# Moving integer weight additions to GpSimd and reordering the first pass of a fused attention and MLP kernel

## The chip, the cores and the metric

The kernel runs on one core of one Trainium2 chip. The metric is the device time of one execution in microseconds, as the median of several executions. A ratio is the mean time of one kernel's runs over the mean of the other's in the same rounds, so it is not quite the ratio of the medians beside it. Different sessions ran on different chips, and the kernel before had a median between 1010.2 and 1012.8 us on them; compare ratios, not medians, across sessions.

Engines: PE is TensorE, PEld its weight loads, DVE is VectorE, ACT is ScalarE, POOL is GpSimd. Tiles whose names end in `_ps` lie in PSUM, the others in SBUF, the two on-chip memories that the program uses. A TensorE pass is one matmul instruction; a slot is one step of TensorE's list, eight such passes in the first matmul, which start 1.73 us apart when nothing holds them up.

## The reference, cut to what matters

```python
kv  = einsum('bhsd,bhse->bhde', k, v)              # q, k, v: 8 x 8 x 576 x 64
o   = einsum('bhsd,bhde->bhse', q, kv)
x   = o / rms(o) * g_norm                          # reshaped to 4608 x 512
h   = x @ w_in                                     # 512 x 2048
g   = s * relu(h)**2 + b
out = g @ w_out                                    # 2048 x 512
```

The two weights arrive as 64-bit floats. The kernel turns them into 32-bit floats on the chip, in its first pass over the tokens.

## The kernel before: the parts that matter here

The tokens go through nine passes, `u = 0` to 8. Both matrix products are done with seven half-size products each (a Strassen scheme), so sums of weight blocks and of activations are needed. Only the first pass also converts weights, 16 blocks of 128 x 1024 words: ScalarE goes over a block twice (fold the high word, round the low one), VectorE shifts the high words and adds the low ones as integers.

```python
def shift_hi(i, dst):
    nc.vector.tensor_scalar(out=dst.bitcast(U32), in0=pairs(i)[:, :, 1],
                            scalar1=3, scalar2=None, op0=ALU.logical_shift_left)

def add_lo(i, dst):
    d = dst.bitcast(U32)
    nc.vector.tensor_tensor(out=d, in0=d, in1=pairs(i)[:, :, 0], op=ALU.add)
...
def join(n):                       # directly one after the other
    shift(n); plus(n)              # plus: add_lo, then send the next load
    if n >= FC // 2: column_sums(s - NS, lower)     # w_out: bias row
    elif lower: [sums() for sums in sums_w_in(s)]   # w_in: Strassen sums
...
# one unit of the first matmul: a result leaves PSUM through ScalarE and VectorE
def z2():
    mm1_product(2, u, s, ps, True)
    t = g_tile("a11")
    add(t, ps, st["r1"])           # VectorE, one input in PSUM, one in SBUF
    relu_sq(t)                     # VectorE, both inputs in SBUF
```

The w_out blocks alternate between upper and lower half, so the second matmul's first product, which needs only the upper half, comes after nearly all of them. The second matmul of the first pass starts with the rows `x1`; the first product there is called "the w_up product" below.

## Time and profile before

| | before |
|---|---|
| median of 3 runs | 1010.23 us (1010.13 to 1012.59) |
| span of the profiled run | 1009.0 us |
| w_up product starts | 97.99 us (12 of 32 TensorE passes), the rest from 103.62 us |
| z2 of the second token pass starts | 167.01 us |
| from there to the end | 842.0 us |

How to read it: the last row is the same in every kernel of this study (841.8 to 842.1 us), because TensorE has no gaps there. So the kernel's span is its second-pass start plus 842.0 us, and all that can change is how soon the first pass ends. The lines that show this are in the prediction.

### The profile page before, as it was taken

The numbers are of one execution on the slowest core, as the hardware profiler recorded it, in microseconds if no ns is written. First come the engines' busy times: TensorE is split into PE (matmuls) and PEld (weight loads), VectorE is DVE, ScalarE is ACT, GpSimd is POOL, SyncE is SP. The second block draws the span as 40 slices with busy tenths as digits, with TensorE's granted clock in tenths as the row PEclk, the third lists the DMA queues.
The fourth block names the chain that finished last, engine by engine and source line by source line (L and its number), as shares of the span: only waits on it lengthen the run. The fifth ranks groups of instructions, "written<-read, shape, count | busy, mean of one in ns | idle before, by whom it ended". The sixth has DMA issues, their size and how long they took to land.

```text
span 1009.0 us, 13489 instructions
## 1 busy us (share of the span) xinstructions
PE 969.8 (96%) x5794; PEld 850.8 (84%) x5794; DVE 459.4 (46%) x749; ACT 205.3 (20%) x354; POOL 1.6 (0%) x8
## 2 busy tenths in 40 slices
PE   4878899999999999999999999999999999999998
PEld 3657688888888888888888888888888888888887
DVE  1989853453344433452445234533453344433441
ACT  2646121212121112112121212021212111112100
POOL 0000000000000000000000000000000000000000
PEclk9989999999999999999999999999999999999999
DMA  9555945913253324522552265134303250323033
GB/s 251 173 193 197 265 152 116 252 67 129 81 134 90 125 73 138 134 98 84 153 136 84 84 167 136 43 125 126 84 6 134 72 165 1 125 73 136 1 125 83
DMA packets 75243, 121.46 MB, mean 120 GB/s; under 512 B 41904, under 2 KB 49072, under 8 KB 68016
## 3 DMA queue, kind: packets, MB, share of 16 engines
q1 hardware_dynamic: 72048, 118.90, 39.2%
q10 hardware_dynamic: 3136, 1.71, 0.8%
q8 instruction: 45, 0.74, 0.3%
q14 instruction: 14, 0.11, 0.0%
HBM read 103.81 MB, written 16.78 MB: 120 GB/s over the span
## 4 chain that ended last, share of the span: by engine, by line
PE 89%; DVE 6%; DMA 2%; ACT 2%; issue 1%; SPq 0%; DVEq 0%; ACTq 0%
PE x_ps L84 49%; PE y_ps L84 26%; PE z_ps L84 8%; PE qT_ps L321 2%; PE kv_ps L297 2%; PE xT_ps L361 1%; DMA kv_sb<-in_k_dram 1%; DVE a L183 1%; DMA w<-w_up 1%; DVE ws L186 1%; DMA q_sb<-in_q_dram 0%; DVE a L409 0%; DVE b_row L183 0%; DVE wb L179 0%; DVE a L186 0%
## 5 line engine op out<-in xcount | busy, mean ns | idle before, releaser
L84 PE MATMUL x_ps<-w_sb,a 128*128 128x256 f32 x768 | 172.3, 379 | 0.0
L84 PEld LDWEIGHTS x_ps<-w_sb,a 128*128 128x128 f32 x768 | 144.3, 190 | 18.9 <-issue 0.2
L84 PE MATMUL x_ps<-xs,ws 128*128 128x256 f32 x576 | 139.1, 385 | 11.2 <-ACT r L425 9.3
L84 PE MATMUL y_ps<-w_sb,a 128*128 128x256 f32 x640 | 143.4, 379 | 0.0
L84 PE MATMUL y_ps<-xs,wb 128*128 128x256 f32 x576 | 136.1, 379 | 0.0
L84 PEld LDWEIGHTS x_ps<-xs,ws 128*128 128x128 f32 x576 | 110.4, 192 | 28.3 <-ACT r L425 10.9
L84 PEld LDWEIGHTS y_ps<-w_sb,a 128*128 128x128 f32 x640 | 119.4, 190 | 15.2 <-issue 0.2
L425 ACT COPY r<-x_ps 128x512 f32<-128x512 f32 x108 | 63.3, 586 | 338.4 <-PE x_ps L84 323.2
L84 PEld LDWEIGHTS y_ps<-xs,wb 128*128 128x128 f32 x576 | 109.3, 190 | 15.1 <-DVE a L183 0.2
L183 DVE TENSOR_TENSOR a<-y_ps,r 128x512 f32<-128x512 f32 x72 | 49.5, 687 | 127.6 <-ACT r L425 127.5
L409 DVE SCALAR_TENSOR_TENSOR a<-a 128x512 f32<-128x512 f32 x108 | 74.8, 692 | 3.7
L84 PE MATMUL x_ps<-xT,wa 128*128 128x256 f32 x288 | 69.5, 385 | 0.2 <-DVE wa L179 0.2
L84 PE MATMUL x_ps<-xT,ws 128*128 128x256 f32 x288 | 68.9, 382 | 0.7 <-ACT r L425 0.7
L84 PE MATMUL z_ps<-xT,wa 128*128 128x256 f32 x288 | 68.0, 379 | 0.0
L497 DVE SCALAR_TENSOR_TENSOR or<-x_ps,s_col,b_row 128x256 f32<-128x256 f32 x54 | 25.9, 482 | 85.9 <-PE x_ps L84 85.9
L347 DVE TENSOR_REDUCE ss<-xn 128x8 f32<-128x512 f32 x36 | 24.6, 684 | 84.6 <-ACT xn L345 84.4
L84 PEld LDWEIGHTS x_ps<-xT,wa 128*128 128x128 f32 x288 | 55.9, 194 | 8.5 <-DVE wa L179 0.6
L458 DVE TENSOR_TENSOR a<-a 128x512 f32<-128x512 f32 x36 | 24.9, 692 | 82.0 <-ACT a L457 82.0
L84 PEld LDWEIGHTS x_ps<-xT,ws 128*128 128x128 f32 x288 | 54.1, 190 | 8.9 <-ACT r L425 1.1
L84 PEld LDWEIGHTS z_ps<-xT,wa 128*128 128x128 f32 x288 | 54.6, 190 | 7.4
L84 PE MATMUL x_ps<-w_sb,s 128*128 128x256 f32 x256 | 57.8, 380 | 0.0
L84 PEld LDWEIGHTS x_ps<-w_sb,s 128*128 128x128 f32 x256 | 47.6, 190 | 6.1 <-issue 0.2
(79 smaller groups left out, 770.2 us busy)
## 6 DMA issues: line engine op xcount, KB each, us to landing
w_sb<-w SPq DMA_DIRECT2D x56, 1024.0 KB, 4.9
kv_sb<-in_k_dram SPq DMA_DIRECT2D x32, 288.0 KB, 5.7
out_dram<-o SPq DMA_DIRECT2D x72, 128.0 KB, 2.3
q_sb<-in_q_dram SPq DMA_DIRECT2D x68, 128.0 KB, 5.5
w_raw<-in_moe_w_in_dram SPq DMA_DIRECT2D x8, 1024.0 KB, 6.4
w_raw<-in_moe_w_out_dram SPq DMA_DIRECT2D x8, 1024.0 KB, 4.9
kv_sb<-in_v_dram SPq DMA_DIRECT2D x28, 288.0 KB, 6.8
w<-w_up SPq DMA_DIRECT2D x4, 1024.0 KB, 7.4
```

The costliest lines, as they stand in the source:

```text
L84: nc.tensor.matmul(o, lhsT=lhsT, rhs=rhs, start=start, stop=stop, skip_group_check=True)
L183: nc.vector.tensor_tensor(out=o, in0=a, in1=b, op=ALU.add)
L186: nc.vector.tensor_tensor(out=o, in0=a, in1=b, op=ALU.subtract)
L297: nc.tensor.matmul(ps[r][l * HB : l * HB + HB, i, :], lhsT=kv[rows, 0, l, j, :], rhs=kv[rows, 1, l, j, :], start=(j == 0), stop=(j == R - 1),)
L321: nc.tensor.transpose(ps[:, p, :], q_in[c][:, 2 * p : 2 * p + 2, :], ident)
L347: nc.vector.reduce_sum(ss, st["xn"], axis=mybir.AxisListType.X)
L361: nc.tensor.transpose(ps[:, p, :], st["xn"][:, 2 * p : 2 * p + 2, :], ident)
L409: nc.vector.scalar_tensor_tensor(t, t, 0.0, t, ALU.max, ALU.mult)
L425: nc.scalar.copy(st[name], src)
L458: nc.vector.tensor_mul(t, t, t)
L497: nc.vector.scalar_tensor_tensor(o, ps, s_col, other, ALU.mult, ALU.add)
```

## The change

The intent: VectorE is the busiest engine of the first pass, and GpSimd does nothing. The change gives GpSimd 14 of the 16 integer adds; loads the upper half of w_out first and brings forward a product that needs only that half (`early_5`); computes the sums of the first pass as they come up rather than in a lump; orders the first loads so that q arrives between the halves of k and v and turns q there; and copies those turned q tiles with VectorE instead of ScalarE. The core of the diff, with cuts:

```diff
-    def add_lo(i, dst):
+    def add_lo(i, dst, engine):
         if wide:
             d = dst.bitcast(U32)
-            nc.vector.tensor_tensor(out=d, in0=d, in1=pairs(i)[:, :, 0], op=ALU.add)
+            engine.tensor_tensor(out=d, in0=d, in1=pairs(i)[:, :, 0], op=ALU.add)
...
-    blocks = conv_order() + [FC + i for i in conv_order()]
+    blocks = [i for s in range(NS) for i in (2 * s, NU + 2 * s)]
+    blocks += [FC + 2 * s for s in range(2 * NS)]
...
     def plus(n):
-        add_lo(blocks[n], place(n))
+        add_lo(blocks[n], place(n), nc.vector if n < 2 else nc.gpsimd)
         send_w()
...
-    for i in range(2):
-        load_kv(0, i, kv0p, (nc.sync, nc.scalar), tag="kv")
-    load_q(0)
-    load_q(2, nc.scalar)
+    both = (nc.sync, nc.scalar)
+    load_kv(0, 0, kv0p, both, tag="kv")
+    load_q(0, both)
+    load_kv(0, 1, kv0p, both, tag="kv")
+    load_q(2, both)
...
-    turn[0]()
-    turn[1]()
+    kv_product(0, lambda: [turn[c]() for c in range(2)])
...
-    turn_x[2]()
     first[0]["x1"]()
+    turn_x[2]()
+    first[0]["z2"]()
     turn_x[3]()
...
-    for sums in (t12, s12, t34, s34):
-        sums()
+    s12()
+    t12()
+    shift(2)
+    plus(2)
+    t34()
+    s34()
...
+    for n, slot in starts.items():
+        at(slot, (hi, n))
+        at(slot + 1, (lo, n), (shift, n), (plus, n))
+        at(slot + 4, (more, n))        # the sums that use block n, three slots later
...
+        if u == 0:
+            return [
+                lambda: x1(0),
+                seq(lambda: x1(1), s2),
+                lambda: early_5(0),
+                lambda: early_5(1),
+                seq(lambda: z2(0), with_bias),
+                ...
```

More of the change, by code (lines that the diff above doesn't have):

```diff
@@ L107, in halves, with load_q @@
         return [(b, i), (b, 4 + i)]
-    def load_q(c, queue=nc.sync):
+    def load_q(c, queues=(nc.sync, nc.sync)):
         t = qp.tile([P, 2, H, D], FP32, name="q_sb", tag="q")
@@ L113, in load_q @@
             for s, (b, j) in enumerate(halves(c + i)):
-                queue.dma_start(
+                queues[i].dma_start(
                     out=t[s * HB : s * HB + HB, i],
@@ L230 @@
     W2_AT = {
-        1: w_up[:, :, :HN], 6: w_up[:, :, :HN], 5: w_up[:, :, :HN], 7: w_up[:, :, HN:],
+        1: w_up[:, :, :HN], 7: w_up[:, :, :HN], 5: w_up[:, :, HN:],
         2: w_dn[:, :, :HN], 4: w_dn[:, :, :HN], 3: w_dn[:, :, HN:],
@@ L247, in column_sums, with sub_w_out @@
                 add(b_row, b_row, w[:, f])
-    def sum_w_out(i, fn, a, b):
-        for s in range(NS):
+    def sub_w_out(i, a, b, steps=range(NS)):
+        for s in steps:
             blocks = slice(2 * s, 2 * s + 2)
-            fn(W2_AT[i][:, blocks], W2_AT[a][:, blocks], W2_AT[b][:, blocks])
+            sub(W2_AT[i][:, blocks], W2_AT[a][:, blocks], W2_AT[b][:, blocks])
     def store_w2(*which):
@@ L285, in bias_row, with kv_product @@
         nc.scalar.copy(b_row, ps)
-    def kv_product(b):
+    def kv_product(b, between=lambda: None):
         ps = [ps_t.tile([P, 2, D], FP32, name="kv_ps", tag="t") for _ in range(2)]
         for i in range(2):
+            if i == 1:
+                between()
             kv = kv_in.pop((b, i))
@@ L318, in turn @@
         def turn():
-            ps = ps_t.tile([P, NP, P], FP32, name="qT_ps", tag="t")
+            if first and c == 0:
+                ps = ps_a.tile([P, NP, P], FP32, name="qT_ps", tag="x")
+            elif first and c == 1:
+                ps = bank_of("att", "z", 1).rearrange("p b (m n) -> p (b m) n", m=2)
+            else:
+                ps = ps_t.tile([P, NP, P], FP32, name="qT_ps", tag="t")
             for p in range(NP):
@@ L322, in turn @@
             st["qT"] = attp.tile([P, NP, P], FP32, name="qT", tag="qT")
-            nc.scalar.copy(st["qT"], ps)
+            if first:
+                nc.vector.tensor_copy(out=st["qT"], in_=ps)
+            else:
+                nc.scalar.copy(st["qT"], ps)
         def product():
@@ L459, in x3 @@
             g_tile("s1")
-            if u > 0:
-                g_sums(s)
+            g_sums(s)
         def y4():
@@ L524, in x1, with early_5, with_bias @@
                 part("r1", j, st["x", j], b1)
-        def first_parts():
-            if u == 0:
-                bias_row()
-                for j in range(2):
-                    part("r1", j, st["x", j], b1)
+        def early_5(j):
+            ps = half(("w", j), "y")
+            product(5, j, ps, True)
+            nc.scalar.activation(rows("o1", j)[:, HN:], ps, AF.Copy, scale=s_col)
+        def with_bias():
+            bias_row()
+            for j in range(2):
+                part("r1", j, st["x", j], b1)
+            for j in range(2):
+                add(st["o1", j][:, HN:], st["o1", j][:, HN:], b2)
+            scaled(st["o1", 0][:, :HN], st["z"], st["r1", 0])
         def z2(j):
@@ L534, in z2 @@
             product(2, j, ps, True)
-            scaled(rows("o1", j)[:, :HN], ps, st["r1", j])
+            if u == 0 and j == 0:
+                st["z"] = ps
+            else:
+                scaled(rows("o1", j)[:, :HN], ps, st["r1", j])
         def s2():
@@ L547, in x6 @@
             part("r2", j, st["x", j], b1)
+            if u == 0:
+                part("r4", j, st["x", j], st["o1", j][:, HN:])
         def y7(j):
@@ L551, in y7 @@
             product(7, j, st["y", j], True)
+            if u == 0:
+                scaled(rows("o2", j)[:, HN:], st["y", j], st["r4", j])
         def x5(j):
@@ L559, in x3 @@
             product(3, j, st["x", j], False)
-            scaled(rows("o1", j)[:, HN:], st["x", j], b2)
+            scaled(rows("o1", j)[:, HN:], st["x", j], b2 if u > 0 else st["o1", j][:, HN:])
             store("o1", j, 4 * u + j)
@@ L577, in nxt, with t3 @@
                 return (lambda: load_w2(u + 1, n - 7)) if u + 1 < U else (lambda: None)
-            return (lambda: None) if u == 0 else (lambda: load_w2(u, n))
-        def t2():
-            if u == 0:
-                sum_w_out(6, add, 7, 1)
-                store_w2(6)
-        def t4():
-            if u == 0:
-                sum_w_out(4, sub, 2, 6)
-                store_w2(4)
-        def t1():
-            if u == 0:
-                sum_w_out(5, sub, 3, 6)
-                store_w2(5)
+            return lambda: load_w2(u, n)
+        def t3():
+            sub_w_out(7, 6, 1)
+            store_w2(7)
+        def t4():
+            sub_w_out(4, 2, 6)
+            store_w2(4)
+        if u == 0:
+            return [
[4 more added lines that the diff above has]
+                seq(lambda: z2(0), with_bias),
+                seq(lambda: z2(1), t3, s4),
+                lambda: x6(0),
+                seq(lambda: x6(1), t4),
+                lambda: y7(0),
+                lambda: y7(1),
+                lambda: x3(0),
+                lambda: x3(1),
+                lambda: y4(0),
+                lambda: y4(1),
+            ]
         return [
             lambda: x1(0),
-            seq(lambda: x1(1), nxt(2), first_parts, t2, s2),
+            seq(lambda: x1(1), nxt(2), s2),
             lambda: z2(0),
-            seq(lambda: z2(1), nxt(3), s4, t4),
+            seq(lambda: z2(1), nxt(3), s4),
             lambda: x6(0),
-            seq(lambda: x6(1), nxt(4), t1),
+            seq(lambda: x6(1), nxt(4)),
             lambda: y7(0),
@@ L606, in mm2 @@
             lambda: x3(0),
-            seq(lambda: x3(1)),
+            lambda: x3(1),
             lambda: y4(0),
-            seq(lambda: y4(1)),
+            lambda: y4(1),
         ]
@@ L618, in tc_late @@
         late["kv"] = ctx.enter_context(tc.tile_pool(name="kvp", bufs=2, side="right"))
-    def conv_order():
-        return [i for s in range(NS) for i in (2 * s, NU + 2 * s)]
-    blocks = conv_order() + [FC + i for i in conv_order()]
+    blocks = [i for s in range(NS) for i in (2 * s, NU + 2 * s)]
+    blocks += [FC + 2 * s for s in range(2 * NS)]
     sent = [0]
@@ L629, in send_w, with where @@
             sent[0] += 1
+    def where(n):
+        return divmod(n, 2) if n < 2 * NS else divmod(n - 2 * NS, NS)[::-1]
     def place(n):
-        s, lower = divmod(n, 2)
-        return w_in_at(s, lower) if n < FC // 2 else w_out_at(s - NS, lower)
+        s, lower = where(n)
+        return w_in_at(s, lower) if n < 2 * NS else w_out_at(s, lower)
     def hi(n):
@@ L639, in lo @@
         round_lo(blocks[n])
-    def split(n):
-        hi(n)
-        lo(n)
     def shift(n):
@@ L648, in plus, with more @@
     def plus(n):
-        add_lo(blocks[n], place(n))
+        add_lo(blocks[n], place(n), nc.vector if n < 2 else nc.gpsimd)
         send_w()
-    def join(n):
-        shift(n)
-        plus(n)
-        s, lower = divmod(n, 2)
-        if n >= FC // 2:
-            column_sums(s - NS, lower)
+    def more(n):
+        s, lower = where(n)
+        if n >= 2 * NS:
+            column_sums(s, lower)
+            if not lower:
+                sub_w_out(5, 5, 1, [s])
         elif lower:
@@ L663 @@
     kv0p = tc.alloc_tile_pool(name="kv0p", bufs=2)
-    for i in range(2):
-        load_kv(0, i, kv0p, (nc.sync, nc.scalar), tag="kv")
-    load_q(0)
-    load_q(2, nc.scalar)
+    both = (nc.sync, nc.scalar)
[3 more added lines that the diff above has]
+    load_q(2, both)
     for _ in range(3):
         send_w()
-    kv_product(0)
-    kv0p.release()
-    gp = ctx.enter_context(tc.tile_pool(name="gp", bufs=NS))
     between = [
@@ L685 @@
     )
-    turn[0]()
-    turn[1]()
+    kv_product(0, lambda: [turn[c]() for c in range(2)])
+    kv0p.release()
+    gp = ctx.enter_context(tc.tile_pool(name="gp", bufs=NS))
     hi(0)
@@ L724, in side_of @@
         if u == 0:
-            side[2].insert(0, lambda: kv_product(1))
+            side = {
+                6: [lambda: kv_product(1)],
+                7: [turn[0]],
+                8: [product[0], turn[1]],
+                9: [turn_x[0], product[1], turn[2]],
+                10: [turn_x[1], product[2], turn[3]],
+                11: [turn_x[2], product[3]],
+                12: [turn_x[3]],
+                13: side[12],
+            }
         return side
@@ L735, in loads, with at @@
             load_q(4 * u + 6)
-    at_slot = {
-        0: [(split, 3)], 1: [(join, 2)], 2: [(join, 3), (split, 4)], 4: [(join, 4), (split, 5)],
-        6: [(join, 5), (split, 6)], 8: [(join, 6)], 9: [(split, 7)], 10: [(join, 7)],
-        12: [(split, 8)], 13: [(join, 8)], 14: [(split, 9)], 15: [(join, 9)], 17: [(split, 10)],
-        18: [(join, 10)], 19: [(split, 11)], 20: [(join, 11)], 21: [(split, 12)],
-        22: [(join, 12)], 23: [(split, 13)], 25: [(join, 13), (split, 14)], 27: [(join, 14)],
-    }
+    at_slot = {}
+    starts = {3: 1, 4: 4, 5: 6, 6: 9, 7: 11, 8: 14, 9: 16, 10: 19, 11: 21, 12: 24, 13: 26}
+    def at(n, *steps):
+        at_slot.setdefault(n, []).extend(steps)
+    for n, slot in starts.items():
+        at(slot, (hi, n))
+        at(slot + 1, (lo, n), (shift, n), (plus, n))
+        at(slot + 4, (more, n))
+    last_slot = 7 * NS
+    at(last_slot, (hi, 14), (lo, 14), (shift, 14), (plus, 14))
+    at(last_slot + 1, (hi, 15), (lo, 15), (shift, 15), (plus, 15))
     for u in range(U):
@@ L763 @@
         for n, slot in enumerate(slots):
-            if u > 0 or n > 0:
+            if u > 0 or n > 1:
                 slot()
@@ L772 @@
                     load_kv(kv_due[u + 1], i, late["kv"], tag="kv")
-        if u == 0:
-            split(FC - 1)
-            join(FC - 1)
-            for i in range(2):
-                load_kv(1, i, convp, tag="raw", bufs=3)
-            loads(0)
-            store_w2(1, 2, 3)
-            sum_w_out(7, sub, 3, 7)
-            store_w2(7)
-            for s in range(NS):
-                g_sums(s)
         second, side = mm2(u), side_of(u)
@@ L786 @@
             slot()
+            if u == 0:
+                run(at_slot.get(last_slot + n, []))
+                if n == 1:
+                    for i in range(2):
+                        load_kv(1, i, convp, tag="raw", bufs=3)
+                    store_w2(1)
+                    loads(0)
+                    store_w2(5)
+                elif n == 2:
+                    t2 = convp.tile([P, 4 * R * D], FP32, name="w_t2", tag="raw", bufs=3)
+                    W2_AT[6] = t2[:, : FC // 2 * HN].rearrange("p (f n) -> p f n", n=HN)
+                    for i in range(14, 16):
+                        more(i)
+                    sub_w_out(6, 3, 5)
+                    store_w2(3, 2, 6)
             if n == 0 and u > 0:
```

## The prediction

> **What bounds the kernel now.** I read the busy time by stretches first, then TensorE's waits, then the timeline around the longest one, then VectorE's groups. The stretches (columns: window, its length, busy us and instructions of PE, PEld, DVE, ACT, POOL, then granted clock, DMA share, GB/s):
>
> ```profile
> 0.00:35.00 35.00, 18.25 (x223) 16.26 (x224) 10.47 (x20) 15.99 (x28) 1.63 (x8) 1.00 0.84 229
> 35.00:60.00 25.00, 17.33 (x76) 13.81 (x75) 23.42 (x34) 12.36 (x15) 0.00 (x0) 0.94 0.58 195
> 60.00:105.00 45.00, 37.72 (x154) 31.26 (x154) 40.42 (x56) 24.32 (x28) 0.00 (x0) 0.92 0.58 190
> 105.00:125.00 20.00, 18.70 (x224) 15.30 (x223) 16.84 (x29) 2.81 (x7) 0.00 (x0) 0.92 0.98 271
> 125.00:165.00 40.00, 38.24 (x203) 33.75 (x202) 20.44 (x39) 7.39 (x14) 0.00 (x0) 1.00 0.41 126
> 165.00:1004.00 839.00, 839.00 (x4922) 740.32 (x4921) 347.35 (x577) 142.44 (x264) 0.00 (x0) 1.00 0.36 106
> ```
>
> From 165 us on, TensorE is busy 839.00 of 839.00 us at full clock; the change leaves that work as it is, so nothing can be won there. Everything lies in the first pass (165 us), where TensorE is busy 18.25 + 17.33 + 37.72 + 18.70 + 38.24 = 130.2 us and idle 34.8. Some 11 of those are the wait for the first k and v. The clock column adds about 0.06 x 25 + 0.08 x 45 + 0.08 x 20 = 6.7 us lost to a lower clock (a little less, as some of it fell in idle time). So the ceiling is near 35 - 10 + 6 = 31 us, 3% of 1010.
>
> In 35 to 105 us VectorE is the busy engine, 23.42 of 25 and 40.42 of 45 us. TensorE's waits there:
>
> ```profile
> PE kv_ps L297 <- DMA kv_sb<-in_v_dram: 11.9, 2, 11.1
> PE x_ps L84 <- ACT r L425: 10.0, 5, 4.6
> PE xT_ps L361 <- DVE xn L353: 3.2, 3, 1.8
> PE x_ps L84 <- DVE w_up L179: 2.9, 1, 2.9
> ```
>
> ACT is named for 10.0 us, but ACT is only the messenger. The timeline at the longest wait:
>
> ```profile
> 57.52 0.69 DVE L409 SCALAR_TENSOR_TENSOR a<-a 128x512 f32<-128x512 f32 x1
> 58.13 0.68 DVE L183 TENSOR_TENSOR a<-y_ps,r 128x512 f32<-128x512 f32 x1
> 58.85 0.69 DVE L409 SCALAR_TENSOR_TENSOR a<-a 128x512 f32<-128x512 f32 x1
> 58.90 0.59 ACT L425 COPY r<-x_ps 128x512 f32<-128x512 f32 x1 [4.04 <-DVE a L183]
> 59.54 3.78 PE L84 MATMUL x_ps<-xs,ws 128*128 128x256 f32 x8 [4.62 <-ACT r L425]
> ```
>
> ACT itself sat 4.04 us until VectorE had read the old r at 58.13, because VectorE was working off its queue; and the eight passes after the pause took 3.78 us where undisturbed ones start 1.73 us apart. So VectorE's queue is the bound from 35 us to about 130 us. What the change aims at is this group:
>
> ```profile
> L179 DVE CUSTOM_DVE_ANT_0 w_up<-w_raw,w_up 128x2048 uint16<-128x2048 uint16 x4 | 4.9, 1226 | 0.2
> L179 DVE CUSTOM_DVE_ANT_0 w_dn<-w_raw,w_dn 128x2048 uint16<-128x2048 uint16 x4 | 4.9, 1226 | 0.3
> L169 DVE TENSOR_SCALAR wa<-w_raw 128x1024 uint32<-128x1024 uint32 x4 | 2.7, 687 | 0.0
> L183 DVE TENSOR_TENSOR b_row<-b_row,w_dn 128x512 f32<-128x512 f32 x8 | 5.5, 692 | 0.3
> ```
>
> An exact integer add of one weight block costs VectorE 1.226 us, and there are 16.
>
> **What the Trainium skill says.** "GPSIMD Engine Reference", 4.1 Engine selection: a 32-bit integer add there is exact, so the result stays right; 3.1 Elementwise gives 4497 ns for a two-input add of 2048 elements. Half that is an estimate of 2.25 us for a block of 1024. No trace here shows it: GpSimd only runs 1.63 us of setup. "SBUF — State Buffer", Who interferes with whom: a VectorE instruction with two SBUF inputs, or in a 2-port mode, contends with a GpSimd instruction that reads SBUF, and the second to issue "fully blocks". Not testable in this trace, and the main doubt. "VectorE: DVE Perf Modes", the tier table: fp32 tensor_scalar from SBUF runs at 2x. The trace agrees for the shift: 1024 words in 687 ns, against 692 ns for a tensor_tensor of 512; so the shift is a 2-port one. "TensorE: Matmul & The Clock Gate", Part 1: an idle window of about 3.4 us halves the clock. The trace agrees: after the 4.62 us pause the pace fell to 3.78 against 1.89 us for eight passes; 2.38 and 2.88 us pauses were also followed by slow passes.
>
> **The change part by part.**
> 1. *Integer adds.* 14 of 16 leave VectorE: 14 x 1.226 = 17.2 us of its time; on GpSimd 14 x 2.25 = 31.5 us by the estimate, at one block per 2.4 TensorE slots of 1.73 us = 4.1 us. GpSimd itself keeps up. The sums using a block follow three slots (5.2 us) after its add, which tolerates an add of up to some 4 to 5 us.
> 2. *w_out upper half first.* The first product of the second matmul needs only the upper half. Before, lower blocks stand between: three shifts (2.1), three adds (3.7) and six column sums (4.2). After, a lower block's work falls under that product and under the w5 product, moved forward: four products of 3.45 us = 13.8 us of TensorE work that needs no lower block. The w5 subtractions (4 x 0.69 = 2.7) and three units' g sums (6 x 0.69 = 4.1) move in front of it.
> 3. *VectorE's work until the first product can run.* Before, durations between 34.5 and 103.5 us sum to 66.2 us in 69. After, counted off the program from the first z addition: 11 additions from PSUM (7.5), 11 relu-squares (7.6), 3 squares (2.1), 16 w_in sums (11.0), 4 x sums (2.7), 10 shifts (6.9), 8 column sums (5.2), 4 w5 subtractions (2.7), 6 g sums (4.1) = 49.8 us. At the same density that is 49.8 x 69/66.2 = 52 us, so the product starts near 34.5 + 52 = 86.5 us. TensorE's 26 slots from 37.4 give 37.4 + 26 x 1.73 = 82, so both fit together.
> 4. *From there to the next pass.* Fourteen half products (48.3), k^T v (2.3), bias and attention (some 7.5) are 58 us without pauses. TensorE's first pass would end at 144.5 instead of 165.3: **20.8 us won if GpSimd costs VectorE nothing**. Before, the stretch from 103.6 took 61.7 us with about 3 us of waits and 2 of half clock.
> 5. *First loads, q turned inside k^T v, qT copied by VectorE.* The first k^T v half can start perhaps 1 us before 11.1. But ACT's first weight fold waits for its block at 21.39 us and stands before the first Square (22.43) in ACT's order, in both kernels. So little comes through: the four turns off ACT (585 ns each; ACT was full, 5.00 of 5.00 us, in 25 to 30 us) against 4 copies on VectorE of about 0.65 and a z addition and relu-square (1.4 us) placed before the x sums. I count 0, plus or minus 1.5.
>
> **The rivals.**
> *A: the lock is total.* Of the 49.8 us, 42.3 are instructions with two SBUF inputs or in 2-port mode; only the PSUM additions (7.5) can lie beside GpSimd. Ten adds needed before the product take the port 10 x 2.25 = 22.5 us. 42.3 + 22.5 = 64.8, plus part of the 7.5 and handing over: about 68 us, product at 102 to 103 instead of 103.6. The later steps still save 2 to 4 us: 1006 to 1010. With an add of 3 us, 7.5 us more come on top: 1010 to 1016. For it: the skill's sentence. Against it: moving 17 us away to hold the port for 31 would be an odd thing to keep, and three slots of slack fit adds that are delayed but done.
> *B: no contention.* 1010 - 20.8 = 989.5, at best; with a few short waits 990 to 994.
> *C: another engine takes over.* ACT's two passes over a block (1.17 + 1.16 us) for 14 blocks and about 15 copies at 0.59 are some 42 us in 52: near, but not the bound. Weight loads: a buffer is held for load (6.4 us), two passes (2.3), shift (0.7) and add (2.25), 11.7 us; three buffers give one block per 3.9 us, just under 4.1. If adds stretch to 4 us it becomes 4.5 us per block, 12 x 0.4 = 5 us lost, so about 5 of the 20.8 go: 994 to 996.
>
> I expect partial contention, VectorE's 42 us stretched by about a quarter (10 us): 20.8 - 10 = 10.8 won. **999.5 us.** The range is 988 (B, early loads helping) to 1011 (A). Two per cent is 20.2 us, below 990.0: needs B nearly whole, 0.14. Slower than 1030.4 needs adds that stop VectorE far more than their own length: 0.03. Within 2%: 0.83.
>
> **What would show it.** The changed profile should have 14 GpSimd adds near 2.3 us each (start to start within one block), VectorE's 512-element sums still near 0.69 us if there is no lock and 1 to 3 us beside an add if there is; the first w_up product between 87 (B) and 103 us (A); no TensorE wait over 3.4 us and full clock after 40 us; the next pass starting between 145 and 163 us; 839 us unchanged after it. I am wrong if the first Square comes much before 22 us (then the first loads did matter), if adds take over 4 us, or if z2's wait for the last lower block opens a new gap.

## The result, and the profile after

The changed kernel took **1015.13 us** (1014.78 to 1017.43, 4 runs), beside 1010.62 us for the kernel before: ratio 1.0046, 95% interval 1.0026 to 1.0066. A repetition in the last session gave 1.0039 (1.0021 to 1.0057). So it is slower, by under half a per cent: within the 2% that the prediction gave a chance of 0.83, but on the other side of the kernel before. The forecast of 999.5 us and the range 988 to 1011 were both missed.

The two stretches that VectorE bounds, in the changed kernel, with the columns of the prediction's first view:

```profile
35.00:60.00 25.00, 20.03 (x74) 16.09 (x72) 19.44 (x25) 10.38 (x12) 7.80 (x3) 0.80 0.42 132
60.00:105.00 45.00, 33.73 (x128) 27.69 (x129) 44.24 (x50) 20.64 (x24) 18.15 (x7) 0.86 0.52 181
```

From 60 to 105 us VectorE was to be relieved. It is busy 44.24 of 45 us, up from 40.42, but it got through 50 instructions instead of 56. TensorE fell from 37.72 to 33.73 us busy, and its granted clock from 0.92 to 0.86. Busier, with fewer instructions: they must have become longer. TensorE's longest waits for other engines (total, times, longest):

```profile
PE x_ps L84 <- ACT r L435: 11.6, 4, 5.6
PE x_ps L84 <- DVE xs L186: 3.9, 1, 3.9
PE b_ps L84 <- DVE b_row L183: 2.5, 1, 2.5
```

The wait through ScalarE's copies has grown from 10.0 us, and two are new; the 2.9 us for `w_up` and the 1.9 us for `ws` are gone. The 3.9 us for the x sums are not GpSimd's doing: the runs without its adds or without its reads, e1 and e3 below, have them too. The groups of VectorE's instructions show which became longer. First the kernel before, then the changed one (count, busy us, mean ns of one, idle before):

```profile
L409 DVE SCALAR_TENSOR_TENSOR a<-a 128x512 f32<-128x512 f32 x12 | 8.3, 692 | 0.4
L183 DVE TENSOR_TENSOR a<-y_ps,r 128x512 f32<-128x512 f32 x8 | 5.5, 685 | 0.0
L245 DVE COPY b_row<-w_up 128x512 f32<-128x512 f32 x1 | 0.4, 427 | 0.0
```

```profile
L419 DVE SCALAR_TENSOR_TENSOR a<-a 128x512 f32<-128x512 f32 x12 | 15.0, 1253 | 0.4
L183 DVE TENSOR_TENSOR a<-y_ps,r 128x512 f32<-128x512 f32 x8 | 5.5, 684 | 5.3 <-ACT r L435 5.3
L245 DVE COPY b_row<-w_up 128x512 f32<-128x512 f32 x1 | 2.6, 2632 | 0.0
```

The same instruction on the same shapes went from 692 to 1253 ns on average where both inputs are in SBUF, and stayed at 685 where one comes from PSUM. The copy has one input, in SBUF, and lengthened too (the last section comes back to it). The timeline shows the single case (start, duration):

```profile
53.83 0.69 DVE L169 TENSOR_SCALAR wa<-w_raw 128x1024 uint32<-128x1024 uint32 x1
...
54.43 0.69 DVE L468 TENSOR_TENSOR a<-a 128x512 f32<-128x512 f32 x1
54.65 2.73 POOL L179 TENSOR_TENSOR wa<-wa,w_raw 128x1024 uint32<-128x1024 uint32 x1 [7.47 <-DVE wa L169]
55.15 2.77 DVE L183 TENSOR_TENSOR s<-a,a 128x512 f32<-128x512 f32 x1
...
57.96 0.69 DVE L186 TENSOR_TENSOR a<-a,a 128x512 f32<-128x512 f32 x1
```

GpSimd's add runs from 54.65 to 57.38 us. The VectorE sum that starts during it, normally 0.69 us, takes 2.77 us and ends at 57.92. The profile counts the blocked time as busy. How it reaches TensorE is seen a little later:

```profile
92.46 0.68 DVE L183 TENSOR_TENSOR a<-z_ps,r 128x512 f32<-128x512 f32 x1
92.68 2.37 POOL L179 TENSOR_TENSOR w_up<-w_up,w_raw 128x1024 uint32<-128x1024 uint32 x1 [6.58 <-DVE w_up L169]
93.18 2.42 DVE L419 SCALAR_TENSOR_TENSOR a<-a 128x512 f32<-128x512 f32 x1
95.53 0.68 DVE L183 TENSOR_TENSOR a<-y_ps,r 128x512 f32<-128x512 f32 x1
...
96.29 0.59 ACT L435 COPY r<-x_ps 128x512 f32<-128x512 f32 x1 [5.66 <-DVE a L183]
...
96.93 3.78 PE L84 MATMUL x_ps<-xs,ws 128*128 128x256 f32 x8 [5.59 <-ACT r L435]
```

The relu-square at 93.18 is held until the add is done; so the addition at 95.53 is late by 2.42 - 0.69 = 1.7 us, so ScalarE may overwrite r late, and TensorE, which has waited 5.59 us, runs its next eight passes in 3.78 us in place of 1.89. Only a part of the 5.59 us belongs to GpSimd: at the same place e1, with all adds on VectorE, waits 5.7 us, and e3, without GpSimd's reads, 3.2. A long VectorE queue is enough for such a wait; the lock is one way to get one. The PSUM addition at 92.46, under which the add started, kept its 0.68 us.

Summed over the groups of the first pass, VectorE's instructions lengthened by 25.8 us: relu-squares 15.0 - 8.3 = 6.7, bias-row sums 9.7 + 6.9 - 5.5 - 4.8 = 6.3, g sums (6.9 - 2.8) + (4.9 - 2.8) + (4.7 - 2.5) = 8.4, x sums 2.2, one copy 2.2. Thirteen of the 14 adds caused it, 1.5 to 2.2 us each; the one at 44.81 us fell into a time when VectorE was idle. The adds taken away were worth 14 x 1.226 = 17.2 us, so VectorE is 8.6 us worse off than with the adds themselves.

### The profile page after: what moved, and what is told of

Its sections match the earlier page's. It is cut to its first block, busy times and chain, and to the rows that moved or that the text cites. A ratio compares the mean times of both kernels' runs of the same rounds, so it can differ in the third digit from the quotient of the medians.

```text
span 1013.3 us, 13513 instructions
## 1 busy us (share of the span) xinstructions
PE 973.7 (96%) x5794; PEld 854.3 (84%) x5794; DVE 470.9 (46%) x741; ACT 204.5 (20%) x352; POOL 38.2 (4%) x22
## 4 chain that ended last, share of the span: by engine, by line
PE 89%; DVE 7%; DMA 2%; issue 1%; ACT 1%; ACTq 0%; DVEq 0%
PE x_ps L84 49%; PE y_ps L84 27%; PE z_ps L84 8%; DMA q_sb<-in_q_dram 2%; PE kv_ps L299 2%; PE xT_ps L371 1%; PE qT_ps L328 1%; DVE a L419 1%; DVE b_row L183 1%; DVE a L186 1%; DVE s L183 1%; DVE a L183 1%; DVE ws L186 0%; DVE xs L186 0%; DVE a L468 0%
## 5 line engine op out<-in xcount | busy, mean ns | idle before, releaser
L84 PE MATMUL y_ps<-xs,wb 128*128 128x256 f32 x576 | 138.3, 384 | 0.8 <-DVE wb L186 0.8
L84 PEld LDWEIGHTS y_ps<-xs,wb 128*128 128x128 f32 x576 | 110.9, 193 | 16.9 <-DVE wb L186 1.5
L419 DVE SCALAR_TENSOR_TENSOR a<-a 128x512 f32<-128x512 f32 x108 | 81.5, 754 | 3.7
L468 DVE TENSOR_TENSOR a<-a 128x512 f32<-128x512 f32 x36 | 27.1, 752 | 78.2 <-ACT a L467 78.2
```

Of the source, the lines that this page charges most:

```text
L84: nc.tensor.matmul(o, lhsT=lhsT, rhs=rhs, start=start, stop=stop, skip_group_check=True)
L419: nc.vector.scalar_tensor_tensor(t, t, 0.0, t, ALU.max, ALU.mult)
L468: nc.vector.tensor_mul(t, t, t)
```

## The experiments

Two milestones are read from each timeline, next to the ratio: when the w_up product starts, and when z2 of the second token pass starts. They come from one profile each; that of the changed kernel's repetition, e13, lies 1.3 to 1.5 us before the first one, so differences of that size between two rows mean nothing.

| run | ratio to before (95%) | w_up product | second pass z2 | span |
|---|---|---|---|---|
| before | 1 | 97.99, most from 103.62 | 167.01 | 1009.0 |
| changed | 1.0046 (1.0026 to 1.0066) | 107.11 | 171.45 | 1013.3 |
| e13_after_again | 1.0039 (1.0021 to 1.0057) | 105.85 | 170.02 | 1011.8 |
| e3_write_only | 0.9858 (0.9841 to 0.9874) | 93.78 | 154.55 | 996.4 |
| e1_all_on_vector | 0.9950 (0.9935 to 0.9965) | 103.33 | 164.14 | 1006.0 |
| e4_old_loads | 1.0031 (1.0016 to 1.0046) | 106.74 | 172.96 | 1014.8 |
| e8_order_alone | 0.9948 (0.9930 to 0.9966) | 100.68 | 163.45 | 1005.4 |
| e6_front_order | 0.9920 (0.9908 to 0.9933) | 96.32 | 159.13 | 1000.9 |
| e10_last_four | 0.9953 (0.9940 to 0.9966) | 97.56 | 165.59 | 1007.4 |
| e12_square_on_scalar | 0.9910 (0.9896 to 0.9923) | 97.36 | 158.14 | 999.9 |

**The theories.** L, the lock: a GpSimd add shuts VectorE out of its second SBUF input for the add's whole length, and since VectorE bounds the first pass, that costs more than the adds did on VectorE. R, the rival: GpSimd's adds cost nothing, and what hurts is the rest, that is the new order, the late bias or the new first loads.

### e1_all_on_vector

```diff
-        add_lo(blocks[n], place(n), nc.vector if n < 2 else nc.gpsimd)
+        add_lo(blocks[n], place(n), nc.vector)
```

> The changed kernel with all 16 integer adds on VectorE; its order is kept. Theory L (the lock): beside the 14 GpSimd adds VectorE's instructions lengthened by 25.8 us in all, where the adds themselves would have cost it 14 x 1.226 = 17.2 us; giving them back wins about 8.6 us in a stretch that VectorE bounds: 1004 to 1009 us, below both kernels. Rival R (the new order of the work, the late bias and the new loads cost the time, GpSimd is innocent): 17 us more on VectorE make it slower than the changed kernel, 1018 to 1030 us.

Measured: 1007.44 us (1006.23 to 1008.48), before 1012.80; ratio 0.9950. This is faster than both kernels although VectorE has 14 adds, 17 us, more to execute. R is refuted: the rest of the change is a gain, and the adds on GpSimd turn it into a loss. The step, 0.0096 x 1011 = 9.7 us by the ratios and 7.3 by the spans, fits the 8.6 us expected from the lengthened instructions.

### e3_write_only

The same GpSimd time, but writes alone. The result is wrong.

```diff
-            engine.tensor_tensor(out=d, in0=d, in1=pairs(i)[:, :, 0], op=ALU.add)
+            if engine is nc.gpsimd:
+                for h in (0, 1, 0, 1, 0):
+                    engine.memset(dst[:, h * 512 : h * 512 + 512], 0.02)
+            else:
+                engine.tensor_tensor(out=d, in0=d, in1=pairs(i)[:, :, 0], op=ALU.add)
```

> Wrong result on purpose. Each of the 14 GpSimd adds is replaced by five GpSimd memsets of 128x512 into the same weight block (about 0.5 us each by the setup's two in 0.99 us, so 2.5 us together), which write SBUF and read nothing; every wait on GpSimd stays. Theory L, in the form that it is GpSimd's reads that shut out VectorE's second input: two-input sums stay at 0.69 us beside it, the first w_up product starts near 87 us and the time is 990 to 996 us, which is what the change would be worth without contention. Rival R (order, GpSimd's own latency): the GpSimd time and the waits on it are the same, so 1010 to 1016 us stay. If instead GpSimd shuts out VectorE whatever it does, also 1010 to 1016, but with VectorE's sums lengthened.

Measured: 998.18 us (996.86 to 999.05); ratio 0.9858. The place that was shown for the changed kernel, in this run's timeline:

```profile
52.27 0.69 DVE L169 TENSOR_SCALAR wa<-w_raw 128x1024 uint32<-128x1024 uint32 x1
...
52.88 0.68 DVE L472 TENSOR_TENSOR a<-a 128x512 f32<-128x512 f32 x1
53.02 2.39 POOL L181 MEMSET wa<- 128x512 f32 x5 [7.60 <-DVE wa L169]
53.59 0.69 DVE L187 TENSOR_TENSOR s<-a,a 128x512 f32<-128x512 f32 x1
54.32 0.69 DVE L190 TENSOR_TENSOR a<-a,a 128x512 f32<-128x512 f32 x1
```

GpSimd is busy 2.39 us, and the sums beside it keep 0.69. TensorE's waits, to be set beside those of the changed kernel:

```profile
PE x_ps L84 <- ACT r L439: 4.1, 3, 3.2
PE x_ps L84 <- DVE xs L190: 3.9, 1, 3.9
```

The wait through r is 4.1 us in place of 11.6, the wait for the bias row is gone, and the one for the x sums has stayed. (One side effect: the memsets no longer read the raw buffer, so its next load does not wait for GpSimd. ScalarE waits 2.9 us for w_out loads here and 5.7 in the changed kernel, so this can be a small part of the gain at most, as far as these waits show it.) GpSimd's presence costs little: VectorE waits 1.2 and 1.0 us for it, and single shifts take 0.82 to 1.02 us. Its reads are what costs. This run is also what the change would be worth without contention: 1.4%, which is 14.4 us by the ratio in the same rounds; by spans, of two sessions, 1009.0 - 996.4 = 12.6 us. It is slightly above the 990 to 996 that I expected; the reason is below.

### e9_one_input

Does it take two operands? Two GpSimd copies with one SBUF input each; only the lowest weight bits are wrong.

```diff
+            if engine is nc.gpsimd:
+                engine.tensor_copy(out=d, in_=d)
+                engine.tensor_copy(out=pairs(i)[:, :, 0], in_=pairs(i)[:, :, 1])
...                                      # else the add, as before
```

> Wrong on purpose in the lowest bits: each GpSimd add is replaced by two GpSimd copies with one SBUF input each (the block onto itself, the high words over the low ones), so GpSimd still reads SBUF, one operand at a time, and all waits and buffers stay as in the changed kernel. If any read by GpSimd shuts out VectorE's second input: VectorE's sums beside the copies lengthen to about the copies' length, ratio 1.000 to 1.008. If only a two-operand read does: sums stay 0.69 us and the ratio is that of e3_write_only, 0.984 to 0.988.

Measured: 1007.68 us (1007.04 to 1009.49); ratio 0.9957 (0.9943 to 0.9971), between the two expected ranges. The timeline at the same place decides:

```profile
52.87 0.68 DVE L472 TENSOR_TENSOR a<-a 128x512 f32<-128x512 f32 x1
53.01 1.44 POOL L180 COPY wa<-wa 128x1024 uint32<-128x1024 uint32 x1 [6.30 <-DVE wa L169]
53.58 1.41 DVE L187 TENSOR_TENSOR s<-a,a 128x512 f32<-128x512 f32 x1
54.40 1.59 POOL L181 COPY w_raw<-w_raw 128x1024 uint32<-128x1024 uint32 x1
55.02 1.51 DVE L190 TENSOR_TENSOR a<-a,a 128x512 f32<-128x512 f32 x1
```

Each copy holds up the VectorE sum that starts during it, to 1.41 and 1.51 us. So a one-input read blocks too. The total is smaller: over the same stretch I count 18 us of lengthening against 26 in the changed kernel, though GpSimd is busy about as long. My reading, not tested, is that a block costs two short waits here in place of one long one, and that VectorE gets a piece of its own work done under each. The expectation was wrong only in its size.

### e5_twice

```diff
+            for _ in range(2 if engine is nc.gpsimd else 1):
                 engine.tensor_tensor(out=d, in0=d, in1=pairs(i)[:, :, 0], op=ALU.add)
```

> Wrong result on purpose: each GpSimd add runs twice on its block. Theory L: each further add shuts VectorE out for another 1.84 to 2.6 us, 14 of them, nearly all in the stretch that VectorE bounds: 1038 to 1052 us. Rival R: an add has three slots, 5.2 us, before its block is used; 5.1 us for two fits, so 1015 to 1022.

Measured: 1045.65 us (1045.28 to 1046.34); ratio 1.0329. (Adding the low words twice stays within the tolerance.) Against the changed kernel's 1.0046 that is 0.0283 x 1012.8 = 29 us for 14 further adds, about 2 us each. Not all of it is the lock: TensorE waits 10.0 us for w_dn blocks whose doubled adds come late (0.6 in the changed kernel). The timeline shows two adds back to back and two VectorE sums held up in turn:

```profile
57.83 5.52 POOL L180 TENSOR_TENSOR wa<-wa,w_raw 128x1024 uint32<-128x1024 uint32 x2 [4.62 <-ACT w_raw L160]
58.33 2.78 DVE L184 TENSOR_TENSOR s<-a,a 128x512 f32<-128x512 f32 x1
61.14 2.76 DVE L187 TENSOR_TENSOR a<-a,a 128x512 f32<-128x512 f32 x1
```

### e4_old_loads and e8_order_alone

e4 is the changed kernel with the first loads, the first two turns and the qT copies as before; e8 is the same on top of e1. The edit of both:

```diff
-    load_kv(0, 0, kv0p, both, tag="kv")
-    load_q(0, both)
-    load_kv(0, 1, kv0p, both, tag="kv")
-    load_q(2, both)
+    for i in range(2):
+        load_kv(0, i, kv0p, both, tag="kv")
+    load_q(0)
+    load_q(2, (nc.scalar, nc.scalar))
...
-            if first:
-                nc.vector.tensor_copy(out=st["qT"], in_=ps)
-            else:
-                nc.scalar.copy(st["qT"], ps)
+            nc.scalar.copy(st["qT"], ps)
...
-    kv_product(0, lambda: [turn[c]() for c in range(2)])
+    kv_product(0)
+    turn[0]()
+    turn[1]()
```

> The changed kernel with the first loads, the place of the first two turns and the qT copies on ScalarE as they were before; GpSimd adds stay. Theory L: this part is worth little either way; x6 started at 39.0 us against 37.4 before, so undoing it gives 0 to 2 us: 1013 to 1015. A theory that the new loads are what made the kernel slower expects 1009 to 1011.

> The new order of the w_out blocks and of the second matmul with all adds on VectorE and with the old first loads, old turns and qT on ScalarE: part two of the change alone (the new order at the start of the first matmul stays too). e4_old_loads showed the loads worth nothing within its noise (1.0031 against 1.0046 of another chip session), so theory: as e1, ratio 0.994 to 0.996. If the early loads matter once GpSimd is out of the way: 0.997 to 0.999.

Measured: e4 1015.49 us (1014.82 to 1016.56), ratio 1.0031, against 1.0046 and 1.0039 for the changed kernel; e8 1007.07 us (1005.22 to 1008.72), ratio 0.9948, against 0.9950 for e1. In both settings the loads and turns are worth nothing that these runs can see. The new order alone is worth half a per cent.

### e7_gpsimd_alone

The first part of the change alone, in the kernel before.

```diff
-            nc.vector.tensor_tensor(out=d, in0=d, in1=pairs(i)[:, :, 0], op=ALU.add)
+            engine = nc.vector if i in blocks[:2] else nc.gpsimd
+            engine.tensor_tensor(out=d, in0=d, in1=pairs(i)[:, :, 0], op=ALU.add)
```

> The kernel before with 14 of its 16 adds on GpSimd and nothing else changed. Its sums stand directly behind the adds, so besides the lock VectorE waits out each add's own 2.4 to 2.7 us. Theory L: each add costs VectorE 2.4 to 2.8 us of blocking or waiting in place of 1.23, 14 x 1.2 to 1.6 = 17 to 22 us, less what falls into VectorE's idle time: ratio 1.010 to 1.022. Without any contention and with the wait alone it would be the same in this order, so this run cannot tell those two apart; it only says what the first part of the change is worth alone. A theory that GpSimd adds are a gain in themselves: below 1.000.

Measured: 1024.23 us (1023.65 to 1025.45); ratio 1.0121 (1.0106 to 1.0137). As said beforehand, this mixes the lock with VectorE's plain wait for each add, and the wait is most of it: VectorE waits 30.1 us for GpSimd in this profile. Alone, the first part costs 1.2%; in the changed kernel, whose sums come later, no such wait is left, but the lock is.

### e6_front_order

From e1: the start of the first matmul put back, so that VectorE does the w_in sums and x sums before it touches the z2 result. The edit, condensed:

```diff
     def z2():
         mm1_product(2, u, s, ps, True)
-        t = g_tile("a11")
-        add(t, ps, st["r1"])
-        relu_sq(t)
+        st["z"] = ps                     # the add and relu_sq in z2_rest,
+        if u > 0 or s > 0: z2_rest()     # called later in the first unit
...
-    first[0]["z2"]()
     turn_x[3]()
+    first[0]["z2"]()
...
-    s12(); t12(); shift(2); plus(2); t34(); s34()
+    for sums in (s12, t12, t34, s34): sums()
+    shift(2); plus(2)
+    first[0]["z2_rest"]()
```

> All adds on VectorE as in e1_all_on_vector, and the start of the first matmul put back: the fourth xn turned before the z2 product, the w_in sums and x sums before the z addition and its relu-square. In e1 as in the changed kernel TensorE waits 3.9 us for the x sums there and then runs some 16 passes at half clock (3.75 and 3.78 us for eight against 1.89), 3.9 + 3.7 = 7.6 us, where the kernel before waits 1.9 us. Theory F (VectorE's order at the start costs time of its own): 3 to 6 us faster than e1, ratio to before about 0.990. Rival: VectorE bounds the stretch until 103 us anyway, so an earlier start is only waited off later: within 1 us of e1, ratio 0.994 to 0.996.

Measured: 1004.43 us (1002.75 to 1005.33, 5 runs); ratio 0.9920 (0.9908 to 0.9933), just clear of e1's interval (0.9935 to 0.9965). TensorE's wait for the x sums was 3.9 us in e1, with the same line as in the changed kernel; in e6:

```profile
PE b_ps L84 <- DVE b_row L183: 1.7, 1, 1.7
...
PE x_ps L84 <- DVE xs L186: 0.6, 1, 0.6
```

The wait shrank from 3.9 to 0.6 us and the w_up product starts 7.0 us earlier (103.33 to 96.32), but only 5.0 us reach the second pass in the profiles (164.14 to 159.13) and 0.3% the time: the bias row, which needs the column sums at the end of VectorE's queue, now makes TensorE wait 1.7 us.

### e10_last_four and e11_first_ten

e6 with only some of the adds on GpSimd.

```diff
-        add_lo(blocks[n], place(n), nc.vector)
+        add_lo(blocks[n], place(n), nc.gpsimd if n >= 12 else nc.vector)        # e10
+        add_lo(blocks[n], place(n), nc.gpsimd if 2 <= n < 12 else nc.vector)    # e11
```

> e6_front_order with only the last four adds (the lower w_out blocks) on GpSimd. They fall under 13.8 us of TensorE work that needs none of them. Theory L with slack: 4 x 1.23 = 4.9 us leave VectorE, some 4 x 1.84 = 7.4 us of lock come on, but in a stretch with slack, so within 2 us of e6: ratio 0.990 to 0.994; the bias wait (1.7 us in e6) grows to at most 4 us. A theory that every GpSimd add costs the same wherever it stands (15.4 us between the changed kernel and one without reads, 14 adds, about 1.1 to 1.4 us each): 4 to 6 us over e6, 0.996 to 0.998.

> The complement of e10_last_four: e6_front_order with adds 2 to 11 on GpSimd, those that stand before the first w_up product, where VectorE bounds. Theory L with slack: net 10 x (1.84 - 1.23) = 6.1 us and more where an add starts under a single short instruction: 5 to 10 us over e6, ratio 0.997 to 1.002. If position does not matter: 10/14 of the difference between changed kernel and e1 (9 us), 6.5 us: 0.998. So this run alone doesn't tell them apart, only together with e10.

Measured: e10 1007.67 us (1005.98 to 1009.19), ratio 0.9953; e11 1008.95 us (1007.36 to 1010.67), ratio 0.9971 (0.9954 to 0.9987). Over e6's 0.9920, measured in another session, that is 0.0033 x 1012 = 3.3 us for the last four adds and 5.2 us for the first ten, each give or take 2 us, so whether the last four cost more apiece is not shown. I expected the last four to hide under TensorE's 13.8 us. They did not. In e10 the product starts at 97.56, close to e6, but TensorE then waits twice:

```profile
PE b_ps L84 <- DVE b_row L183: 2.5, 1, 2.5
PE z_ps L84 <- POOL w_dn L179: 2.1, 1, 2.1
```

In e6 the bias row was waited for 1.7 us and w_dn not at all. VectorE had no slack there to begin with: it is busy 19.14 of 20 us from 105 to 125 us in e6 itself. So the four adds cost their whole net price: the instructions beside them lengthened by 8.6 us (2.79, 3.49, 4.68 and 6.51 us where e6's kind takes 0.69, 1.41, 2.49 and 4.32), and the adds had taken 4 x 1.23 = 4.9. The difference of 3.7 us is near the 3.3 measured. (The 15.4 us in the expectation is 16.9 by the spans of the table.)

### e12_square_on_scalar

e6 with the first pass's four separate squares on ScalarE.

```diff
-            nc.vector.tensor_mul(t, t, t)
+            if u == 0: nc.scalar.activation(t, t, AF.Square)
+            else:      nc.vector.tensor_mul(t, t, t)
```

> e6_front_order with the first pass's four squares of the relu moved from VectorE (0.69 us each, two SBUF inputs) to ScalarE (about 0.6 us each), which has slack: 24 of 45 us busy. If VectorE's queue still bounds the first pass: 4 x 0.69 = 2.8 us less, three of them before the product: 1.5 to 3 us faster than e6, ratio 0.989 to 0.991. If ScalarE's chain takes over: as e6 or slower, 0.992 to 0.994.

Measured: 1002.06 us (1001.76 to 1004.16, 5 runs); ratio 0.9910 (0.9896 to 0.9923). Its interval overlaps e6's, so the step from e6 is not shown to be real; against both the kernel before and the changed one it is clearly faster, and its result is correct. It is the fastest correct kernel here by its mean.

### e13_after_again

> The changed kernel itself, so that it stands on the same chip and beside the same runs of the kernel before as the experiments: 1.0026 to 1.0066, as it was.

Measured: 1016.30 us (1013.24 to 1018.45, 6 runs); ratio 1.0039 (1.0021 to 1.0057), as before.

## Why the prediction was wrong

**What bounds the kernel** was right: from the second pass on nothing changed (841.8 to 842.1 us in every kernel), and VectorE's queue set the first pass.

**Rival A was what happened; the weighing against it was the step that failed.** The prediction says "I expect partial contention, VectorE's 42 us stretched by about a quarter (10 us)". The block is total: beside an add, a two-input VectorE instruction takes 2.2 to 2.9 us instead of 0.69. Twelve of them and a copy lengthened by 25.8 us, 17.4 of it before the product, where the prediction had some 10. The price in time is read off changed kernel against e3_write_only, which differ in GpSimd's reads: product 107.11 - 93.78 = 13.3 us, the stretch from there to the second pass (171.45 - 107.11) - (154.55 - 93.78) = 3.6 us, together 16.9 us, which is the difference of the spans (1013.3 - 996.4); by the ratios it is 0.0188 x 1012 = 19 us. Both reasons given against A were weak. That such a change would be "an odd thing to keep" is a guess on motives, not a reading of the profile. And three slots of slack protect whoever uses the sum, not the engine that is shut out. The Trainium skill's own words ("SBUF — State Buffer", Who interferes with whom), that the second to issue "fully blocks", were quoted and should have carried more weight than either.

**The gain without contention was too large: 20.8 us predicted, 12.6 by e3's span and 14.4 by its ratio.** The failing step is number 3, "At the same density that is 49.8 x 69/66.2 = 52 us". e3's product starts at 93.8, not 86.5. The count of the work was right (e3's VectorE is busy 47.4 us up to its product), but VectorE did not keep its density: it is idle 7.0 us before additions from y_ps, 5.4 of them at 43 to 48 us, because TensorE waited 3.9 us for the x sums and then ran eight passes in 3.75 us; and it waits 2.2 us for GpSimd, in spite of the three slots. The first cause is the z addition and relu-square put before the x sums, which step 5 named (1.4 us) and counted as nothing. e6_front_order shows it to be real: on the all-VectorE kernel, putting that order back moves the product 7.0 us forward and the time by 0.3%.

So 12.6 - 16.9 = -4.3 us in place of +10.8; the spans went from 1009.0 to 1013.3. (By the ratios 14.4 - 19.0 = -4.6.)

**Step 1, the add's own length,** was close: 2.37 to 2.42 us where GpSimd was not held up, 2.70 to 2.73 where it began under a two-input VectorE instruction, 5.53 for the two that began under a shift, against the estimate of 2.25. Rival A was undersized for another reason: its 68 us to the product left VectorE no idle time, where the changed kernel has it busy 65.7 us and idle 6.9 until 107.1; and it counted on 2 to 4 us still being saved afterwards, where contention took another 3.6. That its larger variant, 1010 to 1016, contains the 1015.13 is luck: it rests on adds of 3 us, which did not occur.

**Step 4** was right in the absence of contention: from the product to the second pass's z2, e3 takes 60.8 us; the 58 predicted to the pass's start plus 1.73 for one slot are 59.7.

**Step 5** was right that the loads bring nothing: the first k^T v half began at 8.60 us instead of 11.10, but the second half ended at 19.43 instead of 17.55, and the first Square began at 22.25 instead of 22.43; e4 and e8 show no effect.

**The first matmul's clock.** "No TensorE wait over 3.4 us and full clock after 40 us" failed: waits of 3.9 and 5.6 us remained, and the granted clock was 0.80 and 0.86 in the two stretches up to 105 us. A limit of 3.4 us for one wait does not come out of these traces either: a pause of 2.38 us in the kernel before and one of 3.04 us in the changed one were followed by slow passes (2.74 and 2.69 us for eight), one of 2.88 us in e1 was not (1.99).

**The signs of being wrong** did not warn: the first Square did not come early, no add took over 4 us, and z2 waited 0.57 us for the last lower block. The milestones did: the product at 107.1 us lies outside 87 to 103, and the second pass began about 169.7 us (171.45 less a slot), outside 145 to 163.

What stays open: whether e12's last step is real, and how much of e3's gain comes from its earlier buffer release rather than from the missing reads; the timelines show the unstretched sums directly, and ScalarE's waits for loads differ by only 2.8 us, but no run separates the two in time.

## What to carry to other kernels

In this kernel, work moved off a busy VectorE onto GpSimd was no relief, because GpSimd read SBUF while VectorE needed two SBUF inputs: compare what the GpSimd instruction blocks, not zero, with what it saves (here adds of 2.4 to 2.7 us lengthened VectorE's work by 2.0 us each on average, for 1.23 us saved). Look for the blockage as longer instructions, since the profile shows it as busy time on the victim and a wait on somebody else. When an engine bounds a stretch, the order in which it takes its queue is worth a test of its own (here 0.5% for the new order in e8, 0.3% for doing first, in e6, the sums that TensorE waits for). Whether ScalarE is a better place for spare work is open: the four squares in e12 gave no gain clear of noise.

## What the Trainium skill lacked or had wrong

- "SBUF — State Buffer", Who interferes with whom: nothing wrong. The runs confirm it in size: two-input sums beside an add take 2.77 us instead of 0.69, PSUM additions keep 0.684, sums beside memsets keep 0.69. It speaks of slow-downs, but does not say outright how a profile shows them: as the length of the blocked instruction, not as idle time before it.
- The same section on 2-port instructions: agrees. A VectorE copy of 128x512 in SBUF took 0.427 us alone, 0.714 beside GpSimd memsets and 2.632 beside an add. So here memsets of 0.5 us each (2.39 for five) delayed such an instruction little, and an add by its length. The shifts behave alike: 0.69 us alone, up to 1.02 beside memsets (e3), 1.60 and 1.62 beside GpSimd copies (e9).
- The same section speaks of any GpSimd instruction that reads SBUF, and e9 agrees for a copy with one input: two-input sums took 1.41 and 1.51 us beside copies of 1.44 and 1.59 us. It gives no size for it.
- "GPSIMD Engine Reference", 3.1 Elementwise: half of its figure for 2048 elements, an estimate of 2.25 us, against 2.37 to 2.42 measured for a 1024-word integer add whose second input skips every other word. Its 4.1 Engine selection gives the exact integer add (the results were correct) and calls GpSimd about twice as slow, but not that a neighbour pays: in e5 each further add cost about 2 us of device time, a part of it plain waiting for late blocks.
- "Perfetto Trace Analysis", Optimizing Scalar/DVE Operations, warns that moving work between these two engines "might not help". Here it made the same program 0.9 to 1.0% slower (1.0039 and 1.0046 against 0.9950).
